# Batch 0's attention ahead of the first x @ w_in, in whole head pairs, with later loads for the rest

## The chip, the cores and the metric

The kernel runs on one core of a Trainium2 chip. The metric is the time of one execution on the device, in microseconds (us). A core has five instruction streams that matter here: PE (TensorE, matmuls and transposes), ACT (ScalarE, exp, tanh and copies), DVE (VectorE, elementwise work), POOL (GpSimd, casts), and SP, which here only issues transfers (DMAs). Each stream runs its instructions strictly in the order in which they were written down; streams wait for one another through semaphores.

## The reference

Attention with a sliding window of 128 and four sink keys, over 4 batches x 8 heads x 768 positions x 64 dims, and then a gated two-layer projection of its output:

```python
scores = scale * np.matmul(q, k.transpose(0, 1, 3, 2))
is_sink = pos[None, :] < 4
in_window = (rel >= 0) & (rel < 128)          # rel = query position - key position
scores = np.where(is_sink | in_window, scores, -1e9)
a = softmax(scores)
x = np.matmul(a, v)                            # then heads side by side: 3072 tokens x 512
h = x @ w_in                                   # 512 x 2048
g = h * (1.0 / (1.0 + np.exp(-beta * h)))
out = g @ w_out                                # 2048 x 512, float32
```

Inputs and output are float32; the kernel computes the matmuls in bfloat16. The gate is computed as h * (1 + tanh(beta * h / 2)), with the factor 0.5 applied to the output.

## The kernel before, in words

**Units and superblocks.** The 3072 tokens are cut into eight superblocks T of 384 (TT), half a batch each. A *unit* n (0 to 31) is the attention of one pair of heads (hp = n % 4) in one half batch; superblock T consists of the units 4T to 4T+3. Even superblocks hold half 0 of a batch, odd ones half 1. A half-1 unit also needs keys of half 0 and the sink keys.

**A unit's chain.** `load` (L392) issues the DMAs of q, k and v into staging tiles. `cast` (L438) makes bfloat16 copies on POOL. For units below XBAR = 12, `transpose_in` (L460) transposes q and k on PE, and DVE copies them out of PSUM into qkT (L475); from unit 12 on, SP issues a transposing DMA instead (L453). `sink_keys` (L478) copies the four sink keys of each head into a block-diagonal tile k_sink, two ACT copies, and `scores_sink` (L488) makes their scores and exps for half-1 units. `scores` (L500) makes the windowed scores in two chunks, each with one exp on ACT (L524). For n below ADDED = 4, large negative tiles (far_a, far_b) are added by a matmul with the identity (L509) in place of the mask; above it, `mask` (L528) multiplies the exps by 0 or 1 on DVE. From unit 12 on, `scores_at_once` (L540) and `mask_at_once` (L567) do both chunks in one. `attend` (L575) multiplies by v, and a column of ones beside v gives the row sums; `normalise` (L609) is a reciprocal and a multiplication on DVE. `transpose_out` (L619) brings the result into xT, below unit 12 through PE and a copy, from 12 on by a transposing DMA on SP (L623).

**Projection.** A *hidden step* i (L663) is four matmuls of 384 columns (L651), for one of the 16 blocks of 128 hidden features of a superblock, then tanh on ACT (L659) and the gate on DVE (L672), which writes g[T % 2]. `project` (L678) is g @ w_out: 16 matmuls of 512 columns for each of a superblock's three row blocks (48 in all, L679), a copy (L687 or L691) and the output DMA (L694). The weights come in 16 pieces of 512 KB, eight of w_in and then eight of w_out, through eight staging tiles (`load_w`, L428), and are cast on POOL (`cast_w`, L433).

**PSUM.** There are eight banks: acc0, acc1, h_ps (two), s_ps (four, of which the third is used for transposes, `tr`, and the fourth for attention outputs, `av`). `hidden_bank` (L640) gives the bank of a hidden step: acc0 and acc1 in turn for superblock 0, all of acc0, acc1 and h_ps for superblock 1, the two of h_ps from superblock 2 on.

**The order of the work.** The program is first written as a list of operations: units 0 to 3, then a loop over steps s from -6. Steps 0 to 31 are the hidden steps of superblocks 0 and 1; steps 32 to 47 (S_P0 to S_PIPE) project superblock 0; from 48 on every step has one hidden step of superblock T + 1 and three project matmuls of T. `FIRST[n]` says at which step unit n enters, and STEPS at how many steps behind that its parts stand (sink 1, scores 2 and 3, attend 5, out 7). Casts and loads of later units hang on the same steps. Then `Prog.order` (L153) goes through the list with an estimated duration for each operation and puts it on its engine at the earliest time its estimate allows, looking at most 160 operations ahead (40 for SP); equal times go by the order of the list. Operations marked `line` (the early loads) keep their order among themselves. The model of transfers adds one duration after another at given rates (`transfer`, L342), and an issue on SP always takes 500 ns in it. What it gives is the fixed order of each engine's instructions.

At the start PE runs 21 matmuls on a tile of ones (`keep_busy`, L718), 14 before the first transposes and 7 behind the cast of unit 0's k.

Of the kernel before, what the change touches and what calls it, by code (L numbers as in the profile page):

```python
# [15 lines left out]
D1 = D + 1  # L16
# [54 lines left out]
class Prog:  # L71
# [13 lines left out]
    FIRST_DMA = 2000.0  # L85
# [67 lines left out]
    def order(self):  # L153
# [10 lines left out]
        dma_free = self.FIRST_DMA  # L164

        def best(e):
# [10 lines left out]
            return max(n.ready, free[e]), n  # L177

        while len(placed) < len(self.nodes):
# [3 lines left out]
            if n.dma is None:  # L183
                n.done = start + n.busy + n.lag
            else:

                dma_free = max(dma_free, start + n.busy) + n.lag
                n.done = dma_free + 2000.0
            n.place = start
# [73 lines left out]
def bass_streamingllm_window__then__act_swish_beta_kernel(  # L263
# [42 lines left out]
    mask_b = sb("mask_b", (128, 512), BF16)  # L306
    far_a = sb("far_a", (128, TT), BF16)
# [13 lines left out]
    g = [sb(f"g{z}", (128, NM, TT), BF16) for z in range(2)]  # L321
    out_sb = [sb(f"out_sb{z}", (128, NOUT), F32) for z in range(4)]
# [19 lines left out]
    def transfer(size, rate):  # L342
        return {"busy": 500.0, "lag": size / rate}
# [9 lines left out]
    def constants():  # L353
# [14 lines left out]

        two = mask_b[:, :].rearrange("p (r x) -> p r x", r=2)
# [21 lines left out]

    def load(n, v_queue="sp"):  # L392
        b, hp, half, pb = place(n)
        t0 = half * TT
        if n < XBAR:
            for name, src in (("q", q), ("k", k)):
# [4 lines left out]
                   dma=f"{name}{pb}_{half}", line=n < WHOLE, **transfer(2 * TT * D * 4, 329))  # L401
        halves = (0, 1) if n >= WHOLE else (half,)
        first, size = (0, 6) if n >= WHOLE else (3 * half, 3)
        for name, src in (("q", q), ("k", k), ("v", v)):
            if name != "v" and n < XBAR:
                continue
            for hh in range(2):
# [6 lines left out]
                   **transfer(size * 128 * D * 4, 220))  # L414
# [13 lines left out]
    def load_w(i):  # L428
        view, src, _ = w_piece(i)
        op("sp", lambda e: e.dma_start(view, src), w=[("wst", i % NW)], dma=f"w{i % NW}",  # L430
           line=True, **transfer(1 << 19, 389))
# [6 lines left out]
    def cast(n):  # L438
        _, _, half, pb = place(n)
        z = n % NQK  # L440
# [4 lines left out]
        for x, name in enumerate("qk"):  # L445
            op("gp", lambda e, x=x, name=name: e.tensor_copy(qk16[z][:, x, :, :, :], view(name)),  # L446
# [5 lines left out]
        if n >= XBAR:  # L452
# [3 lines left out]
               r=[("q16", z), ("k16", z)], w=[("qkT", pb, half)], dma=f"t{pb}{half}",  # L456
               **transfer(2 * TT * 256, 150))


    def transpose_in(n, bank=tr_ps, name_of="tr", eng="dve"):  # L460
        _, _, half, pb = place(n)
        bank16 = bank[:, :].bitcast(BF16)
        z = n % NQK
        for which, name in enumerate("qk"):
# [11 lines left out]
           x=[name_of], w=[("qkT", pb, half)], **(act(768) if eng == "act" else dve(865.0)))  # L476

    def sink_keys(n, eng="act"):  # L478
        pb = place(n)[3]
        for hh in range(2):  # L480
            op(eng, lambda e, hh=hh: (e.copy if eng == "act" else e.tensor_copy)(  # L481
                k_sink[pb][64 * hh:64 * hh + 64, HEAD1 * hh:HEAD1 * hh + NSINK],
                qkT[pb][64 * hh:64 * hh + 64, 0, 1, 0:NSINK]),
               r=[("qkT", pb, 0), ("k_sink", pb), ("k_sink2", pb)],
               w=[("k_sink", pb) if hh == 0 else ("k_sink2", pb)],
               **(act(128) if eng == "act" else dve(180.0)))

    def scores_sink(n, bank, name):  # L488
        pb = place(n)[3]
        op("pe", lambda e: e.matmul(bank[:, 0, 0:TT], k_sink[pb][:, :], qkT[pb][:, 1, 0, :],  # L490
                                    start=True, stop=True),
           r=[("k_sink", pb), ("k_sink2", pb), ("qkT", pb, 1)], w=[f"{name}0"], **pe(TT))
        op("act", lambda e: e.activation(E_sink[n % 2][:, :], bank[:, 0, 0:TT], AF.Exp, bias=0.0,
                                         scale=SCALE),
           x=[f"{name}0"], w=[("E_sink", n % 2)], **act(TT))
# [4 lines left out]
    def scores(n, c, bank, name):  # L500
# [11 lines left out]
        with P.together("pe"):  # L512
            for kb, qb, nq in CHUNKS[half][c]:
                w = 128 * nq
                for hh in range(2):
# [5 lines left out]
                       r=[("qkT", pb, half), ("qkT", pb, kb // 3)], w=[f"{name}{hh}"],  # L521
                       busy=50.0 + w / 4.8, lag=260.0)
                at += w
        op("act", lambda e: e.activation(E[n % 2][:, c, :, 0:at], bank[:, 0:2, 0:at], AF.Exp,  # L524
                                         bias=0.0, scale=SCALE),
           x=[f"{name}0", f"{name}1"], w=[("E", n % 2, c)], **act(768))

    def mask(n, c):  # L528
        if n < ADDED:
# [6 lines left out]
            E[n % 2][:, c, :, 0:w], E[n % 2][:, c, :, 0:w],  # L536
            m[:, first:first + w].unsqueeze(1).to_broadcast([128, 2, w]), ALU.mult),
           r=[("E", n % 2, c), *names], w=[("E", n % 2, c)], **dve(466.0))
# [356 lines left out]
```

## Time and profile before

| | us |
|---|---|
| median of 3 runs | 234.16 |
| lowest, highest | 233.91, 235.1 |
| span of the profiled execution | 234.5 |

The profiled execution gives no time of its own beside its span. The span runs from the first to the last instruction of the profile; it lies 0.3 us above the median of the timed runs and inside their spread.

| engine | busy us | share of the span |
|---|---|---|
| PE | 219.4 | 94% |
| ACT | 144.3 | 62% |
| DVE | 135.2 | 58% |
| POOL | 74.3 | 32% |

DMAs moved 39.76 MB, 170 GB/s over the span. The span in 40 slices of 5.86 us, with the busy share of TensorE and of the DMA engines in tenths (9 is 90% or more), the granted clock in tenths, and what was moved in GB/s:

```profile
PE   4996989999969999999999999999999999999994
PEclk9999999999997999999999999999999999999999
DMA  6999999999699999998999886842220112111012
GB/s 158 269 373 264 318 328 227 321 388 197 147 212 226 177 218 255 203 231 201 215 232 214 182 169 164 160 84 64 62 64 17 45 20 62 45 48 45 19 71 89
```

A line of the timeline has the start, the duration, the engine, the line of the kernel, the operation, output<-input, and how many were merged; in brackets stands how long the engine had been idle and what released it. SPq is SP issuing a transfer.

### The profile page before, as it was taken

The page shows a single profiled execution, that of the slowest core. Times are in us where ns is not written, and L with a number is a line of the kernel's source. Part 1 is how long each engine was busy: PE and PEld are TensorE (multiplying, and loading weights), DVE is VectorE, ACT ScalarE, POOL GpSimd, SP SyncE. Part 2 cuts the span into 40 slices and gives each one's busy share as a digit, 9 for nine tenths or more (in the row PEclk, how much of TensorE's full clock was granted, in tenths as well). Part 3 has the DMA queues.
Part 4 walks back from the last instruction along what each step waited for, and adds up shares of the span by engine and source line. Part 5 has one row for each costly group of instructions (what it writes and reads, how often), then busy time and mean ns, then how long its engine had stood idle before and what let it go on. Part 6 is the DMA issues. An engine that isn't in the chain of part 4 may idle for free.

```text
span 234.5 us, 4406 instructions
## 1 busy us (share of the span) xinstructions
PE 219.4 (94%) x1690; PEld 119.7 (51%) x1714; DVE 135.2 (58%) x261; ACT 144.3 (62%) x249; POOL 74.3 (32%) x134
## 2 busy tenths in 40 slices
PE   4996989999969999999999999999999999999994
PEld 2653545555434555544555555555555555555541
DVE  5374999699632645632667547766656665343300
ACT  2385887697506674755875669767775874555421
POOL 7677777598313223214115343410000000000000
PEclk9999999999997999999999999999999999999999
DMA  6999999999699999998999886842220112111012
GB/s 158 269 373 264 318 328 227 321 388 197 147 212 226 177 218 255 203 231 201 215 232 214 182 169 164 160 84 64 62 64 17 45 20 62 45 48 45 19 71 89
DMA packets 96084, 39.76 MB, mean 170 GB/s; under 512 B 82736, under 2 KB 88896, under 8 KB 96064
## 3 DMA queue, kind: packets, MB, share of 16 engines
q1 hardware_dynamic: 93888, 39.07, 71.0%
q10 hardware_dynamic: 1632, 0.40, 0.8%
q8 instruction: 13, 0.21, 0.4%
q0 software_dynamic: 544, 0.02, 0.2%
q14 instruction: 7, 0.06, 0.1%
HBM read 27.30 MB, written 6.29 MB: 143 GB/s over the span
## 4 chain that ended last, share of the span: by engine, by line
PE 68%; SPq 20%; DMA 8%; issue 2%; POOL 1%; ACT 0%; POOLq 0%; ACTq 0%
PE acc L679 32%; PE h_ps L651 27%; SPq L410 13%; DMA v_stage<-in_v_dram 6%; SPq L399 4%; PE s_ps L554 4%; PE s_ps L604 3%; SPq L430 3%; DMA qkT<-qk 1%; PE s_ps L490 1%; PE s_ps L593 1%; PE h_ps L679 1%; POOL v_aug L449 0%; ACT out_sb L687 0%; POOL qk L446 0%
## 5 line engine op out<-in xcount | busy, mean ns | idle before, releaser
L679 PE MATMUL acc<-w_out,g 128*128 128x512 bf16 x345 | 94.0, 382 | 1.3 <-issue 0.5
L659 ACT ACTIVATE th<-h_ps,beta_half 128x384 f32<-128x384 f32 x104 | 58.9, 581 | 37.7 <-PE h_ps L651 35.8
L651 PE MATMUL h_ps<-xT,w_in 128*128 128x384 bf16 x416 | 79.4, 326 | 0.3 <-issue 0.2
L672 DVE SCALAR_TENSOR_TENSOR g<-th,h_ps 128x384 bf16<-128x384 f32 x104 | 56.0, 552 | 33.6 <-ACT th L659 32.0
L651 PEld LDWEIGHTS h_ps<-xT,w_in 128*128 128x128 bf16 x416 | 39.5, 98 | 30.3 <-DVE g L672 1.5
L679 PEld LDWEIGHTS acc<-w_out,g 128*128 128x128 bf16 x368 | 34.7, 98 | 34.0 <-issue 3.8
L570 DVE TENSOR_TENSOR E<-E,mask_all 128x1536 bf16<-128x1536 bf16 x20 | 19.4, 972 | 29.0 <-ACT E L561 29.0
L561 ACT ACTIVATE E<-s_ps 128x1536 bf16<-128x1536 f32 x20 | 28.9, 1447 | 5.9 <-PE s_ps L554 5.7
L446 POOL CAST qk<-q_stage 128x384 bf16<-128x384 f32 x32 | 18.3, 571 | 33.9 <-DMA qkT<-qk 33.3
L449 POOL CAST v_aug<-v_stage 128x384 bf16<-128x384 f32 x32 | 16.6, 529 | 35.0 <-PE s_ps L604 24.7
L687 ACT ACTIVATE out_sb<-acc 128x512 f32<-128x512 f32 x23 | 13.6, 597 | 14.6 <-PE acc L679 14.2
L651 PE MATMUL acc<-xT,w_in 128*128 128x384 bf16 x96 | 19.1, 327 | 2.6 <-DVE g L672 2.0
L604 PEld LDWEIGHTS s_ps<-v_aug,E 128*128 128x128 bf16 x384 | 17.1, 97 | 5.3 <-ACT E L524 0.7
L604 PE MATMUL s_ps<-v_aug,E 128*128 128x65 bf16 x384 | 19.4, 193 | 0.5 <-ACT E L524 0.4
L614 DVE TENSOR_TENSOR o_norm<-s_ps,rden 128x384 bf16<-128x384 f32 x32 | 17.8, 558 | 2.2 <-DVE rden L612 0.5
L446 POOL CAST qk<-k_stage 128x384 bf16<-128x384 f32 x32 | 18.3, 572 | 2.4 <-DMA k_stage<-in_k_dram 1.7
L659 ACT ACTIVATE th<-acc,beta_half 128x384 f32<-128x384 f32 x24 | 13.7, 580 | 5.9 <-PE acc L651 5.3
L672 DVE SCALAR_TENSOR_TENSOR g<-th,acc 128x384 bf16<-128x384 f32 x24 | 12.9, 547 | 3.8 <-ACT th L659 3.7
L524 ACT ACTIVATE E<-s_ps 128x768 bf16<-128x768 f32 x16 | 12.9, 809 | 2.2 <-PE s_ps L517 2.1
L475 DVE COPY qkT<-s_ps 128x768 bf16<-128x768 bf16 x10 | 9.5, 954 | 5.7 <-PE s_ps L468 5.7
L651 PEld LDWEIGHTS acc<-xT,w_in 128*128 128x128 bf16 x96 | 8.1, 98 | 8.5 <-DVE g L672 3.4
L481 ACT COPY k_sink<-qkT 64x4 bf16<-64x4 bf16 x32 | 6.1, 190 | 10.0 <-DVE qkT L475 9.0
(64 smaller groups left out, 155.0 us busy)
## 6 DMA issues: line engine op xcount, KB each, us to landing
out_dram<-out_sb SPq DMA_DIRECT2D x24, 256.0 KB, 2.3
q_stage<-in_q_dram SPq DMA_DIRECT2D x28, 192.0 KB, 4.2
k_stage<-in_k_dram SPq DMA_DIRECT2D x28, 192.0 KB, 4.2
wst<-in_moe_w_in_dram SPq DMA_DIRECT2D x8, 512.0 KB, 6.3
wst<-in_moe_w_out_dram SPq DMA_DIRECT2D x8, 512.0 KB, 9.1
v_stage<-in_v_dram SPq DMA_DIRECT2D x16, 192.0 KB, 4.2
v_stage<-in_v_dram SPq DMA_DIRECT2D x28, 96.0 KB, 5.3
q_stage<-in_q_dram SPq DMA_DIRECT2D x8, 96.0 KB, 3.3
```

The costliest lines, as they stand in the source:

```text
L410: op(v_queue, lambda e, hh=hh, s=s, name=name: e.dma_start(stage[name][pb][:, hh, first:first + size, :], s), w=[(name + "_stage", pb, x, ...
L446: op("gp", lambda e, x=x, name=name: e.tensor_copy(qk16[z][:, x, :, :, :], view(name)), r=[(name + "_stage", pb, half, hh) for hh in range ...
L449: op("gp", lambda e: e.tensor_copy(v_aug[pb][:, 3 * half:3 * half + 3, :, 0:D], view("v")), r=[("v_stage", pb, half, hh) for hh in range(2 ...
L561: op("act", lambda e: e.activation(E[z][:, :, :, :].rearrange("p c h x -> p c (h x)"), s_ps[:, :, :].rearrange("p (h b) x -> p h (b x)", h ...
L570: op("dve", lambda e: e.tensor_tensor(both, both, mask_all[:, half, :].unsqueeze(1).to_broadcast([128, 2, 768]), ALU.mult), r=[("E", z, 0) ...
L604: last=(x == len(kbs) - 1): e.matmul(av_ps[:, at + hh * D1:at + hh * D1 + D1], E[z][:, c, h2, col:col + 128], v_aug[pb][:, kb, hh, :], sta ...
L614: op("dve", lambda e: e.tensor_tensor(o_norm[o][:, :, :, :].rearrange("p m h d -> p (m h) d"), src[:, :, 0:D], rden[z][:, :].unsqueeze(2). ...
L651: op("pe", lambda e: e.matmul(bank, w_in16[:, c, m * 128:(m + 1) * 128], xT[:, c, T * TT:(T + 1) * TT], start=(c == 0), stop=(c == 3)), r= ...
L659: op("act", lambda e: e.activation(th[i % 3][:, :], bank, AF.Tanh, bias=0.0, scale=beta_half[:, m:m + 1]), x=[name], r=["beta"], w=[("th", ...
L672: op("dve", lambda e: e.scalar_tensor_tensor(g[T % 2][:, m, :], th[i % 3][:, :], 1.0, bank, ALU.add, ALU.mult), r=[("th", i % 3)], x=[name ...
L679: op("pe", lambda e: e.matmul(bank, g[T % 2][:, m, t * 128:(t + 1) * 128], w_out16[:, m, :], start=(m == 0), stop=(m == NM - 1)), r=[("g", ...
L687: op("act", lambda e: e.activation(out_sb[z][:, :], bank, AF.Copy, bias=0.0, scale=0.5), x=[name], w=[("out_sb", z)], **act(NOUT))
```

## The change

It regroups the first part of the program and makes everything behind it later by steps.

- **Order of units.** Units 0, 4, 1, 5, 2, 6, 3, 7 (the two halves of each head pair) all run before the first full hidden step. `turn(n)` gives their place, by which E, rden and o_norm are chosen. The loop over steps begins at 0.
- **Whole pairs.** Pair 0 is still loaded and cast by units (0 and 4). Pairs 1 to 3 are loaded whole (`load_pair`: one DMA for q, one for k, two for v), cast whole (`cast_pair`, into the still unused g[1]) and transposed whole (`turn_pair`: all of k in bank tr, all of q in acc0, one DVE copy each).
- **Sink keys.** One POOL multiplication of the four keys by a 0/1 tile `own_head`, in place of two ACT copies, for every pair. Two more selects at the start fill own_head.
- **Hidden steps** of superblocks 0 and 1 go round all four banks. One hidden step is begun before the last part of xT is there, in place of two.
- **Slots.** Units 8 to 11 enter at steps 31, 34, 37 and 40 (before 22, 26, 30, 34), units 12 on two steps later than before. Units 4 to 7 have no slots any more. The last chunk of scores of units 4 to 7 is in h_ps, as for 0 to 3, and their sink scores are in acc1.
- **Loads.** All loads of the first units go through SP (before, the v of units 0 and 1 went through ACT's queue). The order on SP is batch 0, w_in, w_out, units 8 to 13; 14 and 15 hang on the casts of 12 and 13, and whole pairs of batches 2 and 3 are asked for when the unit two before them is cast (before, four before them).
- **Casts.** The eight casts of w_in stand behind the casts of batch 0, those of w_out at step 0, ahead of the casts of units 8 and 9. The two DMAs of the sinks' v stand behind the casts of pair 0's units.
- **The ordering model.** At most seven transfers under way (DEPTH): an eighth issue waits for the landing of the one seven before it. Rates and issue times of transfers are changed, a transposing DMA's issue takes 1250 or 1400 ns in the model, and FIRST_DMA is 1300.
- **keep_busy**: 10 matmuls in place of 21.

The core of the diff:

```diff
-FIRST = {4: -6, 5: -4, 6: -2, 7: 1, 8: 22, 9: 26, 10: 30, 11: 34}
-FIRST.update({n: 42 + 4 * (n - 12) for n in range(12, NU)})
+FIRST = {8: 31, 9: 34, 10: 37, 11: 40}
+FIRST.update({n: 44 + 4 * (n - 12) for n in range(12, NU)})
...
-    FIRST_DMA = 2000.0
+    FIRST_DMA = 1300.0
+    DEPTH = 7
...
+            start = max(n.ready, free[e])
+            if n.dma is not None and len(landing) >= self.DEPTH:
+                start = max(start, landing[-self.DEPTH])
+            return start, n
...
+    def load_pair(hp):
+
+        for name, src in (("q", q), ("k", k)):
+            s = src[0, 2 * hp:2 * hp + 2, :, :].rearrange("h (p c) d -> p h (c d)", c=6)
...
+        for hh in range(2):
+            s = v[0, 2 * hp + hh, :, :].rearrange("(c p) d -> p c d", p=128)
...
+    def cast_pair(hp):
+        z = hp % 2
+        for x, name in enumerate("qk"):
+            op("gp", lambda e, x=x, name=name: e.tensor_copy(
+                pair16[z][x][:, :, :, :], stage[name][hp][:, :, :, :].rearrange("p h c d -> p c h d")),
...
+    def turn_pair(hp):
+        z = hp % 2
+        for x, (bank, name) in ((1, (tr_ps, "tr")), (0, (acc[0], "acc0"))):
+            bank16 = bank[:, :].bitcast(BF16)
+            with P.together("pe"):
+                for c in range(6):
+                    op("pe", lambda e, c=c, x=x, bank16=bank16: nc.tensor.transpose(
...
+            op("dve", lambda e, dst=dst, src=src: e.tensor_copy(dst, src), x=[name],
+               w=[("qkT", hp, half) if x else ("qT", hp, half) for half in range(2)], **dve(865.0))
...
-    def sink_keys(n, eng="act"):
+    def sink_keys(n):
         pb = place(n)[3]
-        for hh in range(2):
...
+        op("gp", lambda e: e.tensor_tensor(
+            k_sink[pb][:, 0:2 * HEAD1].rearrange("p (h x) -> p h x", h=2)[:, :, 0:NSINK],
+            qkT[pb][:, 0, 1, 0:NSINK].unsqueeze(1).to_broadcast([128, 2, NSINK]), own_head[:, :, :],
+            ALU.mult), r=[("qkT", pb, 0), "own_head"], w=[("k_sink", pb)], busy=120.0, lag=100.0)
...
-        k = i % 2 if i < NM else i % 4 if i < S_P0 else 3 - i % 2
+        k = i % 4 if i < S_P0 else 3 - i % 2
...
-    for n in range(4):
-        load(n, "act" if n < 2 else "sp")
+    load(0)
...
     load(4)
...
+    for hp in range(1, 4):
+        load_pair(hp)
+    for x in range(8):
+        load_w(x)
     cast(0)
-    cast(1)
+    cast(4)
...
-    keep_busy(14, 215.0)
...
+    keep_busy(10, 215.0)
+    transpose_in(0)
+    cast_pair(1)
+    transpose_in(4, acc[0], "acc0")
+    for n in (0, 4, 1, 5, 2, 6, 3, 7):
+        hp, half = n % 4, n // 4
+        if half == 0:
+            if 0 < hp < 3:
+                cast_pair(hp + 1)
+            if hp:
+                turn_pair(hp)
+            sink_keys(n)
         scores(n, 0, s_ps, "s")
+        if half == 0 and hp:
+            scores_sink(n + 4, acc[1], "acc1")
...
+        if n == 6:
+            for i in range(8):
+                cast_w(i)
+        if n == 3:
+            for i in range(8, 16):
+                load_w(i)
+            for n_ in range(8, 14):
+                load(n_)
+            with P.together("pe"):
+                for c in range(3):
+                    hidden_matmul(0, c)
...
-    casts = {FIRST[n - 2] + 1: n for n in range(6, NU) if n not in (8, 9)}
-    for s in range(-6, S_END + NM):
+    casts = {FIRST[n - 2] + 1: n for n in range(10, NU)}
+    for s in range(S_END + NM):
...
-            if n >= XBAR and n % 8 >= 4 and n + 4 < NU:
-                load(n + 4)
...
+            if n in (12, 13):
+                load(n + 2)
+            if n >= XBAR + 2 and n % 8 in (6, 7, 0, 1) and n + 2 < NU:
+                load(n + 2)
...
-        if s == FIRST[7] + 1:
+        if s == 0:
 
-            for x in (8, 9, 10, 11):
+            for x in range(8, 16):
                 cast_w(x)
             cast(8)
...
             cast(9)
```

More of the change, by code (lines that the diff above doesn't have):

```diff
@@ L340, in dve, with transfer @@
         return {"busy": t, "lag": 140.0}
-    def transfer(size, rate):
-        return {"busy": 500.0, "lag": size / rate}
+    def transfer(size, rate, issue=525.0):
+        return {"busy": issue, "lag": size / rate}
     def select(out_ap, in_ap, patt, cmp, fill, base, cm, r, w):
@@ L783, in bass_streamingllm_window__then__act_swish_beta_kernel @@
             if step in ("a", "b") and n < XBAR:
-                scores(n, "ab".index(step), *((h_ps, "h") if n < 8 and step == "b" else (s_ps, "s")))
+                scores(n, "ab".index(step), s_ps, "s")
                 later.append(lambda n=n, step=step: mask(n, "ab".index(step)))
```

175 lines of the change are left out of this document (76 added, 99 removed).

## The prediction

> **What bounds the kernel now.** I read the chain that ended last first, as shares and then in order of time; then busy time and clock by stage; then single engines inside the stages.
>
> ```profile
> PE 68%; SPq 20%; DMA 8%; issue 2%; POOL 1%; ACT 0%; POOLq 0%; ACTq 0%
> ```
>
> The chain in order of time:
>
> ```profile
> 45.02 1.21 SPq L410
> 46.27 1.73 SPq L410
> ...
> 58.38 1.48 SPq L410
> 66.60 3.48 DMA qkT<-qk
> 71.21 0.85 PE acc L679 x2
> ```
>
> Up to 70 us the end hangs on SP's queue and the transfers (the 28%); from 71 us on it hangs on TensorE alone. Columns of the next view: stretch in us, its length, then busy us (instructions) of PE, PEld, DVE, ACT, POOL, then granted clock, DMA share, GB/s.
>
> ```profile
> 8.70:19.00 10.30, 9.48 (x120) 5.78 (x119) 6.19 (x11) 8.69 (x19) 6.56 (x10) 1.00 1.13 324
> 19.00:42.00 23.00, 19.73 (x202) 11.26 (x199) 20.05 (x40) 16.02 (x29) 16.77 (x26) 1.00 1.03 283
> 42.00:56.00 14.00, 13.60 (x107) 7.91 (x105) 12.18 (x25) 12.34 (x25) 12.16 (x17) 1.00 1.01 325
> 56.00:67.86 11.86, 11.70 (x104) 5.95 (x105) 8.34 (x17) 4.80 (x10) 5.46 (x11) 1.00 0.77 172
> 67.86:70.12 2.26, 0.00 (x1) 0.00 (x0) 0.36 (x1) 0.00 (x0) 0.11 (x1) 1.00 1.23 228
> 70.12:74.80 4.68, 4.67 (x20) 1.72 (x21) 0.46 (x1) 2.17 (x3) 1.03 (x3) 0.64 1.30 229
> 74.80:234.50 159.70, 154.88 (x1123) 83.66 (x1142) 84.56 (x157) 98.81 (x165) 25.86 (x48) 1.00 0.60 125
> ```
>
> The last row is the pipelined part: 97% PE, full clock. It starts when the projection of superblock 0 is done, at 74.80. So the change is worth what it moves that boundary, plus what it breaks behind it. Ahead of the boundary time is lost in three places: 19 to 42 us (superblock 0's hidden steps, among attention, round two banks), the PE gap of 2.26 us, and the half clock behind the gap (mean 0.64 over 4.68 us). The gap on PE:
>
> ```profile
> 67.53 0.33 PE L631 MATMUL s_ps<-ident,o_norm 128*128 128x128 bf16 x3
> 70.13 0.34 PE L490 MATMUL s_ps<-qkT,k_sink 128*128 128x384 bf16 x1 [2.27 <-DMA qkT<-qk]
> ```
>
> PE waits for unit 12's transposing DMA, which SP issued only at 66.60, behind a row of loads. SP puts later output transposes off too:
>
> ```profile
> 66.60 1.32 SPq L453 DMA_TRANSPOSE qkT<-qk  x1
> ...
> 93.89 1.26 SPq L623 DMA_TRANSPOSE xT<-o_norm  x1
> ```
>
> Unit 12's o_norm was written at 77.06 to 77.62, so its transpose stood 16 us in SP's queue. Unit 19's was ready at 120.4 and issued at 132.28; superblock 4's hidden matmuls begin at 137.77, and 96.7 us follow from there.
>
> ACT in a unit of the first stage:
>
> ```profile
> 14.33 0.42 ACT L481 COPY k_sink<-qkT 64x4 bf16<-64x4 bf16 x2
> 14.75 0.81 ACT L524 ACTIVATE E<-s_ps 128x768 bf16<-128x768 f32 x1
> 15.46 0.81 ACT L524 ACTIVATE E<-h_ps 128x768 bf16<-128x768 f32 x1
> 16.15 0.49 ACT L635 COPY xT<-acc 128x384 bf16<-128x384 bf16 x1
> 16.69 0.42 ACT L481 COPY k_sink<-qkT 64x4 bf16<-64x4 bf16 x2
> ```
>
> There is no gap: 2.36 us a unit, and ACT sets it.
>
> **The change, part by part.** Durations are distances between starts where instructions follow closely.
>
> *All attention of batch 0 first (stage A).* Four pairs, each a half-0 and a half-1 unit. Per pair: ACT four exps at 0.70, one sink exp 0.37, two copies at 0.5: 4.2. The two key copies (0.42) go; with them it would be 4.6. DVE: two copies into qkT at 0.87, two reciprocals and normalisations at 0.70, two masks at 0.47 (31.31, POOL idle beside it) to 0.92 (26.68, beside a POOL cast): 4.1 to 5.0. PE: half 0 0.34 in, 0.66 far tiles, 0.54 scores, 0.57 attend, 0.17 out; half 1 0.34, 0.16 sink, 0.54, 0.62, 0.17: 4.1. POOL: two casts of 384 columns lie 0.45 apart, so 0.9 for a 768-column one, three of them, and the key multiplication: 2.9. Three engines stand at 4.1 to 5.0, so I take 4.75, nearer DVE's upper end, since POOL casts through all of the stage. From the first qkT copy (8.62, left there) four pairs end at 27.6. The last unit's transposes and ACT copy add 1.2 (20.02 to 20.87 is 0.85, and a wait): 28.8. Superblock 0 needs only the seventh unit, 2.4 earlier, while PE still owes 1.8 to the eighth: PE is free for hidden steps from about 28.3.
>
> *Loads of the stage.* Batch 0 is 4.72 MB; the trace moved 4.69 MB by 17.6 us (158, 269, 373 GB/s), so pair 3 lands near 17.7, about 5 us before its turn. w_in, 4.19 MB at the next slices' 264 to 328, is in by 31.5; its last quarter is needed twelve steps (7.8) after 28.3, which leaves 3.6 for the cast of 1.04. The v loads of units 0 and 1 move from ACT's queue to SP's, four issues of 0.5, but whole pairs need 20 loads where there were 32: SP is 8 issues (4 us or more) better off. The pieces of q and k double in length; no gain is counted for that.
>
> *Start.* Two more selects on POOL, 0.3 to 0.45 each, lie ahead of its 0.84 us wait for the v_sink fill: 0. The v_sink DMAs (1.36 us of POOL) may now follow the casts: 0 to 1.4 earlier or later for the first cast; 0. Eleven of 21 filler matmuls go. Those of 256 columns came 0.213 us apart between 5.61 and 7.74 (0.83 ns a column, later matmuls 0.42), so the array was at half speed until about 8.4. With less filler this may last. Nothing lost if not; if through all of pair 0, 4.1 of PE becomes 8.2 against 4.75: 3.4. I take 1.0, as the recorded half-clock stretch at 70 us (3.4 us long, so 1.7 lost) is nearest, and part of it lies beside waits for loads.
>
> *Key multiplication on POOL.* Not in the trace: between 0.10 (memset of 1 column) and 0.35 (128 columns); 0.25. One a pair, POOL at 2.9 of 4.75 covers it. It waits for a DVE copy with the next pair's casts behind it; these have about 1.8 us a pair to spare. Uncovered it is 4 x 0.25 = 1 us.
>
> *x @ w_in round four banks.* 32 steps of four matmuls, 0.65 a step in the dense rows (46.49 to 49.09 is four steps in 2.60): 20.8. ACT (0.48) and DVE (0.47) stay under it. Before, superblock 0's sixteen steps, with four units, took 19 to 42 us. I add 0.5 at the start, where banks are still shared with the last unit.
>
> *Projection of superblock 0, now with units 8 to 11 whole.* 48 x 0.216 = 10.4; units at 0.34 + 0.54 + 0.45 + 0.17 = 1.5, four: 6.0; unit 12's sink and scores 0.9: 17.3. Such a mix ran with 0.16 us free in 11.86 (56.00 row); I add 0.5. What would be late next are the loads: w_out, 4.19 MB behind w_in at 321 to 388, is in near 44; units 8 to 12, 2.95 MB at 230 to 260, near 56. Unit 8 enters near 49, its load in by 46.5 and cast by 48.5, behind w_out's casts on POOL; unit 12's transpose can go at 58, its scores come near 66. The gap and its half clock have 8 us of cover.
>
> *Loads and slots later.* Units 12 on start two steps later in a program that stands earlier: a whole pair is asked for eight steps before its cast (16 before), about 13 us at 1.65 a step. Landing took 4 to 9 us in this trace, so 0; without the cover, see the second rival. SP's transposes no longer stand behind the loads of units 24 to 27. PE work behind the boundary is the same: 159.7.
>
> Sum: 28.3 + 1.0 + 20.8 + 0.5 + 17.3 + 0.5 + 159.7 = 228.1 of span against 234.5. The median (234.16) lies 0.3 under this span, so about **228.0**. With ends: stage A at 4.1 or 5.7 a pair, start 0 to 3.4: 224.2 to 234.0 (225.2 with the 1.0 kept).
>
> A rule of the Trainium skill about the gap: TensorE: Matmul & The Clock Gate, "What's actually happening", gives an idle window of about 3.4 us ahead of half rate. Here 2.27 us were enough, and the row decides. By the page only the gap itself would be saved, an estimated 1.7 us less.
>
> **The rivals.**
> 1. Stage A is slower: the pair's chain runs through four engines, and a pair at 5.7 with 2 us of half speed gives 28.3 + 3.8 + 2.0 + 198.8 - 0.3 = 232.6. For it: masks at 0.92 beside POOL. Against: units followed at 2.36 with ACT full.
> 2. The other side: late loads move the wait to superblock 4. It cannot start before unit 19's output is transposed, and 96.7 us follow. Units 12 to 19 need 6.6 us each; unit 12 is done near 69.5, unit 19 near 116. A whole pair is 1.18 MB per four steps; the slice at 59 to 64 us moved 147 GB/s, 8.0 us a pair. At 8.5 a unit the last ends near 137.5, superblock 4 starts near 142, and the end is at 238.4. It decides from about 7.8 a unit. For it: DMA share over 1 from 70 to 100 us. Against: units came every 6.1 us there, with loads for units 24 to 27 between them.
> 3. No gain: DMA keeps its pace, units 12 to 19 end when they did, and PE's lead is spent waiting: 233 to 235.
> 4. The clock falls through the hidden steps. Rotating through banks leaves small pauses on PE; if half of the 20.8 us ran at half clock, +10: 238. Against: 42 to 56 us, already round four banks, held 1.00. The page named above states this in "A second HAM failure mode: psum-queue depth-cycling"; the trace does not bear it out.
>
> **How the numbers follow.** Forecast 0.52 (225.5 to 231.5); better, pairs at 4.2 and no half clock, 0.10 (223 to 225.5); rival 1 0.15; rival 3 0.07; rival 2 0.12; rival 4 0.04. Under 233.0 is faster by 0.5%, about what a measurement can tell: faster 0.77, same 0.07, slower 0.16. The range 223.5 to 235.0 leaves out the slower ones and a little of the better case.
>
> **What would show it.** Right: projection of superblock 0 ends near 68 to 69, the 32 hidden steps take about 21 us from 28 to 29, no PE gap over 1 us before 70 us, and 159 to 160 us follow. Wrong: PE waiting for xT at superblock 3 or 4, half clock in the first 30 us, pairs over 5.5 us.

## The result, and the profile after

| | before | after |
|---|---|---|
| median (lowest to highest), us | 234.03 (233.84 to 235.1) | 242.35 (239.43 to 243.29) |
| span of the profiled execution, us | 234.5 | 241.4 |
| superblock 0's hidden steps begin in full, us | 19.0 | 33.2 |
| projection of superblock 0 ends, us | 74.8 | 74.0 |
| from there to the end, us | 159.7 | 167.4 |

The change made the kernel slower: ratio 1.027 [1.021, 1.034], against a forecast of 228.0 and a range of 223.5 to 235.0. The ratio goes by the two faster of the four runs (239.43 and 241.58); the profiled execution is one of the other two (243.12). All profiled executions from here on have a time of their own, 1.7 to 2.0 us above their span.

So both halves of the forecast failed: the boundary came 0.8 us earlier, not 6.4, and what follows became 7.7 us longer. First the windows of after, cut at its own stages (columns as before: stretch, length, busy us and instructions of PE, PEld, DVE, ACT, POOL, then clock, DMA share, GB/s):

```profile
8.70:33.20 24.50, 20.28 (x247) 13.10 (x246) 18.08 (x30) 16.59 (x27) 19.44 (x29) 1.00 1.09 366
33.20:55.36 22.16, 22.16 (x133) 13.05 (x131) 17.13 (x32) 18.02 (x32) 13.77 (x19) 0.92 0.94 278
55.36:74.00 18.64, 18.55 (x171) 9.12 (x168) 13.82 (x28) 8.83 (x13) 8.52 (x19) 1.00 0.65 126
74.00:101.40 27.40, 27.40 (x226) 15.09 (x225) 16.07 (x29) 18.23 (x27) 9.81 (x20) 1.00 1.16 238
101.40:137.00 35.60, 30.32 (x215) 15.23 (x214) 17.16 (x32) 19.21 (x28) 8.39 (x18) 0.93 0.84 196
```

The rows are batch 0's attention, the 32 hidden steps of superblocks 0 and 1, the projection of superblock 0 with units 8 to 11, and then the pipeline. The last row is where the pipeline loses: PE is idle for 5.28 of 35.60 us, and the clock is 0.93. Before, no stretch behind the boundary looked like this. The timeline of PE in after names the two waits:

```profile
103.58 0.99 PE L709 MATMUL h_ps<-xT,w_in 128*128 128x384 bf16 x5 [1.48 <-DMA xT<-o_norm]
133.16 1.78 PE L709 MATMUL h_ps<-xT,w_in 128*128 128x384 bf16 x5 [3.80 <-DMA xT<-o_norm]
```

At superblock 3 and again at superblock 4, the first hidden step has its first three matmuls done and stands before the fourth, whose part of xT has not landed. Behind the second wait five matmuls take 1.78 us instead of 0.99: half clock, granted for 6.8 us from 132.3 on. Lost are 1.48 + 3.80 in waits and, of the 6.8, what lies behind the wait at half speed, (6.8 - 0.86) / 2 = 3.0: 8.3 together, where the pipeline grew by 7.7. (It is no full balance: behind the boundary PE was idle for 4.8 us before and for 8.5 after.)

Why the part of xT was late is in SP's queue, of after:

```profile
119.27 1.22 SPq L681 DMA_TRANSPOSE xT<-o_norm  x1
...
122.22 1.53 SPq L444 DMA_DIRECT2D v_stage<-in_v_dram  x2
123.80 1.86 SPq L444 DMA_DIRECT2D q_stage<-in_q_dram  x2
125.71 1.40 SPq L444 DMA_DIRECT2D k_stage<-in_k_dram  x2
127.15 1.30 SPq L444 DMA_DIRECT2D v_stage<-in_v_dram  x2
128.49 2.61 SPq L681 DMA_TRANSPOSE xT<-o_norm  x1
```

and in DVE's timeline:

```profile
122.19 0.56 DVE L672 TENSOR_TENSOR o_norm<-s_ps,rden 128x384 bf16<-128x384 f32 x1
```

This is unit 19's o_norm. It was ready at 122.75, but its transpose stood 5.7 us behind issues of loads for batch 3, went out at 128.49 and landed 4.6 us later. (The chain of waits links this transpose to an o_norm that starts at 128.34. That is unit 20's, and it ends at 128.90, after the issue at 128.49: a releaser that ends later than what it is said to release is a wrong guess, and the queue's own view tells the truth.)

The transpose was late only for this order of PE. In before it went out 3.8 us later than here, at 132.28, after 11.9 us in the queue; but PE came to superblock 4 only at 137.6, with more project matmuls ahead of it, and didn't wait. In after PE stood there from 129.4 on.

### The profile page after: what moved, and what is told of

The parts are those of the page before. It is cut to its first block, busy times and chain, and to the rows that moved or that the text cites. A ratio compares the mean times of both kernels' runs of the same rounds, so it can differ in the third digit from the quotient of the medians.

```text
span 241.4 us, 4374 instructions
## 1 busy us (share of the span) xinstructions
PE 224.4 (93%) x1703; PEld 121.8 (50%) x1703; DVE 137.4 (57%) x257; ACT 141.6 (59%) x221; POOL 74.2 (31%) x143
## 4 chain that ended last, share of the span: by engine, by line
PE 86%; DVE 6%; DMA 3%; ACT 3%; issue 1%; DVEq 0%; ACTq 0%
PE acc L737 34%; PE h_ps L709 31%; PE s_ps L662 5%; PE acc L709 4%; PE s_ps L612 4%; DMA xT<-o_norm 3%; ACT E L582 2%; DVE E L593 2%; PE s_ps L575 1%; PE h_ps L737 1%; PE s_ps L651 1%; DVE o_norm L672 1%; PE s_ps L529 1%; PE s_ps L548 1%; DVE v_sink L360 1%; PE s_ps L567 1%
## 5 line engine op out<-in xcount | busy, mean ns | idle before, releaser
L717 ACT ACTIVATE th<-h_ps,beta_half 128x384 f32<-128x384 f32 x112 | 64.6, 581 | 59.6 <-PE h_ps L709 57.4
L737 PE MATMUL acc<-w_out,g 128*128 128x512 bf16 x368 | 99.0, 381 | 0.1
L709 PE MATMUL h_ps<-xT,w_in 128*128 128x384 bf16 x448 | 90.1, 334 | 5.3 <-DMA xT<-o_norm 5.3
L730 DVE SCALAR_TENSOR_TENSOR g<-th,h_ps 128x384 bf16<-128x384 f32 x112 | 61.4, 552 | 51.1 <-ACT th L717 48.8
L709 PEld LDWEIGHTS h_ps<-xT,w_in 128*128 128x128 bf16 x448 | 44.1, 100 | 42.7 <-DMA xT<-o_norm 6.1
L737 PEld LDWEIGHTS acc<-w_out,g 128*128 128x128 bf16 x368 | 33.4, 98 | 31.2 <-issue 3.7
L507 POOL CAST qk<-q_stage 128x384 bf16<-128x384 f32 x26 | 13.7, 528 | 44.8 <-DMA q_stage<-in_q_dram 26.4
L582 ACT ACTIVATE E<-s_ps 128x768 bf16<-128x768 f32 x16 | 13.1, 818 | 18.0 <-PE s_ps L575 17.3
L662 PEld LDWEIGHTS s_ps<-v_aug,E 128*128 128x128 bf16 x384 | 17.6, 99 | 6.6 <-DVE E L593 1.7
L672 DVE TENSOR_TENSOR o_norm<-s_ps,rden 128x384 bf16<-128x384 f32 x32 | 17.8, 557 | 1.1
L507 POOL CAST qk<-k_stage 128x384 bf16<-128x384 f32 x26 | 14.4, 553 | 12.4 <-DMA k_stage<-in_k_dram 12.3
L709 PE MATMUL acc<-xT,w_in 128*128 128x384 bf16 x64 | 12.6, 339 | 0.0
L670 DVE RECIPROCAL rden<-s_ps 128x6 f32<-128x6 f32 x32 | 6.1, 191 | 8.8 <-PE s_ps L662 8.6
L612 PE MATMUL s_ps<-qkT 64*128 64x256 bf16 (+2 forms) x144 | 10.4, 261 | 0.0
L651 PE MATMUL s_ps<-v_sink,E_sink 128*128 128x130 bf16 x48 | 9.7, 226 | 0.5 <-ACT E_sink L551 0.5
```

Of the source, the lines that this page charges most:

```text
L507: op(eng, lambda e, x=x, name=name: e.tensor_copy(qk16[z][:, x, :, :, :], view(name)), r=[(name + "_stage", pb, half, hh) for hh in range( ...
L582: op("act", lambda e: e.activation(E[turn(n) % 2][:, c, :, 0:at], bank[:, 0:2, 0:at], AF.Exp, bias=0.0, scale=SCALE), x=[f"{name}0", f"{na ...
L612: op("pe", lambda e, kb=kb, bank=bank, qb=qb, at=at, nq=nq, rows=rows: e.matmul(s_ps[:, bank, 128 * at:128 * (at + nq)], qkT[pb][rows, kb ...
L662: last=(x == len(kbs) - 1): e.matmul(av_ps[:, at + hh * D1:at + hh * D1 + D1], E[z][:, c, h2, col:col + 128], v_aug[pb][:, kb, hh, :], sta ...
L672: op("dve", lambda e: e.tensor_tensor(o_norm[o][:, :, :, :].rearrange("p m h d -> p (m h) d"), src[:, :, 0:D], rden[z][:, :].unsqueeze(2). ...
L709: op("pe", lambda e: e.matmul(bank, w_in16[:, c, m * 128:(m + 1) * 128], xT[:, c, T * TT:(T + 1) * TT], start=(c == 0), stop=(c == 3)), r= ...
```

## The experiments

Each is compared with runs of the kernel before on the same chip. Times in us; the ratio is to before, with a 95% interval.

**1. The old numbers of the ordering model in the changed kernel (e1_transfer_model_before).** Kernel: the changed one, all else kept.

```diff
-    FIRST_DMA = 1300.0
-    DEPTH = 7
+    FIRST_DMA = 2000.0
+    DEPTH = 9999
...
-    def transfer(size, rate, issue=525.0):
+    def transfer(size, rate, issue=500.0):
+        issue, rate = 500.0, {240: 150, 280: 150, 250: 220, 300: 329, 330: 329, 380: 389, 350: 389}[rate]
```

> The changed kernel with the ordering model's transfer numbers of the kernel before (no DEPTH, 150 GB/s for transposing DMAs, 500 ns an issue); program list unchanged. Order theory (the fixed PE order puts the first hidden steps of superblocks 3 and 4 just where the model lets xT land, and the real landing is 10 to 14 us behind the model, so PE waits 1.5 and 3.8 us and then runs 6.8 us at half clock): with these numbers the projection of superblock 3 comes ahead of superblock 4's hidden steps, the two waits go, the part from superblock 2's first hidden step to the end falls from 167.3 to 159 to 161 us, total near 234 to 236. Transfer theory (loads of batches 2 and 3 take the time they take, whatever the order): the waits only move, total 239 to 244.

Measured: 234.6, ratio 1.0016 [0.9975, 1.0056], span 232.8. No wait for xT, no half clock; boundary 72.3, then 160.5. The whole slowdown goes with these numbers, though they execute nothing: they only decide where instructions stand. Counted in the traces, 192 project matmuls stand ahead of superblock 4's first hidden step in e1 and 158 in after. The 34 that moved behind it are 34 x 0.216 = 7.3 us of work that could have run while PE waited there for 3.8 us; that the count decides is argued here, and experiment 7 speaks against it. SP's queue alone doesn't decide either. In e1:

```profile
116.48 0.56 DVE L673 TENSOR_TENSOR o_norm<-s_ps,rden 128x384 bf16<-128x384 f32 x1
...
125.70 3.56 SPq L682 DMA_TRANSPOSE xT<-o_norm  x2
...
135.65 1.47 PE L710 MATMUL h_ps<-xT,w_in 128*128 128x384 bf16 x8
```

Unit 19's o_norm was done at 117.04 and its transpose, the first of the two, went out at 125.70. It stood 8.7 us in the queue, longer than the 5.7 of after, and PE didn't wait, since it came to superblock 4 only at 135.65.

**2. No loads of batch 3 (e2_no_batch3_loads).** The changed kernel:

```diff
-            if n >= XBAR + 2 and n % 8 in (6, 7, 0, 1) and n + 2 < NU:
+            if n >= XBAR + 2 and n % 8 in (6, 7, 0, 1) and n + 2 < 24:
```

> The changed kernel without the loads of batch 3 (units 24 to 31 compute on batch 2's q, k and v again; this leaves out 4.7 MB of transfers). Both the order theory and the transfer theory expect unit 19's output transpose to be issued 4 to 6 us sooner (no loads ahead of it in SP's queue) and the wait at superblock 4 to shrink from 3.8 us to under 1, with its half clock: total 234 to 237. The slot theory (units stand two steps too late, loads have no part) expects the wait to stay at 3 us or more and the total within 2 us of 241.

Measured: 236.34, ratio 1.0034 [0.9996, 1.0073]. Unit 19's transpose went out at 122.42, right behind its o_norm, and the wait at superblock 4 is gone. The one at superblock 3 stayed (1.99 us at 101.73, then half clock):

```profile
122.42 1.19 SPq L681 DMA_TRANSPOSE xT<-o_norm  x1
...
101.73 1.07 PE L709 MATMUL h_ps<-xT,w_in 128*128 128x384 bf16 x5 [1.99 <-DMA xT<-o_norm]
```

So it is those loads that unit 19's transpose stands behind. Their transfers are gone as well as their issues, so this run doesn't say which of the two held it up.

**3. The filler matmuls back (e3_filler_back).** The changed kernel:

```diff
-    keep_busy(10, 215.0)
+    keep_busy(14, 215.0)
     transpose_in(0)
+    keep_busy(7, 200.0, [("k16", 0)])
```

> The changed kernel with the 21 filler matmuls of the kernel before (14, and 7 behind the cast of unit 0's k). Order and transfer theories: half speed ends near 9 us in place of 16.3, the attention of batch 0 ends 1 to 3 us sooner (superblock 0's hidden steps begin near 31 in place of 33.2), but unit 19's output lands only 0 to 1.5 us sooner, so the wait at superblock 4 grows and the total falls by less than 1.5. Start theory (the slow start is what costs): total falls by 3 us or more.

Measured: 240.08, ratio 1.0187 [1.0103, 1.0271]; full clock from 7.3 us (16.3 in after), yet the full hidden steps start at 32.9 (33.2 in after), not near 31, and those of superblock 1 at 42.9; in e2, at full clock only from 13.7, they start at 42.6. Half speed in the first pairs costs next to nothing. The wait at superblock 4 didn't grow, as expected, but shrank to 2.55 us, with 3.4 us of half clock behind it, and the median fell by 2.3: both misses. What e3 saves against after ahead of the boundary (superblock 1's steps start at 45.0 there) is another stretch: in after, half clock is granted for 3.4 us from 33.4, 1.7 us lost just as the dense matmuls begin; e3 and e2 don't have it.

**4. Loads of whole pairs four units ahead again (e4_early_pair_loads).** The changed kernel:

```diff
-            if n >= XBAR + 2 and n % 8 in (6, 7, 0, 1) and n + 2 < NU:
-                load(n + 2)
+            if n >= XBAR and n % 8 >= 4 and n + 4 < NU:
+                load(n + 4)
```

> The changed kernel with the rule of before for whole-pair loads (asked for when the unit four before them is cast, in place of two). If it is the lateness of these loads that makes units 12 to 19 late: unit 19's output transposed 3 us sooner or more, total 236 to 238. If the loads stand in SP's queue ahead of the output transposes either way (order and transfer theories): unit 12's and 13's outputs are transposed later than now (83.2 and 90.5), unit 19's about where it is (within 2 us of 128.5), total 240 to 244.

Measured: 241.71, ratio 1.0255 [1.016, 1.0349], with waits for xT of 1.23 and 3.67 us; unit 12's transpose went out at 92.4, unit 19's at 129.9. The change of when loads are asked for isn't the cause.

**5. The kernel before with only the new numbers (e5_before_with_new_model).**

```diff
-    FIRST_DMA = 2000.0
+    FIRST_DMA = 1300.0
+    DEPTH = 7
...
+            if n.dma is not None and len(landing) >= self.DEPTH:
+                start = max(start, landing[-self.DEPTH])
...
-               **transfer(2 * TT * 256, 150))
+               **transfer(2 * TT * 256, 240, 1400.0))
...
-               r=[("o_norm", z)], w=[("xT", T, hp)], dma=f"x{z}", **transfer(TT * 256, 150))
+               r=[("o_norm", z)], w=[("xT", T, hp)], dma=f"x{z}", **transfer(TT * 256, 280, 1250.0))
```

and the rates of loads, weights and output as in the change.

> The kernel before with only the changed kernel's transfer numbers in its ordering model (DEPTH 7, the new rates and issue times, FIRST_DMA 1300); units, loads, slots and banks as before. In the order that comes out, 109 and 151 project matmuls stand ahead of the first hidden steps of superblocks 3 and 4 on PE (138 and 188 in the kernel before, 107 and 158 in the changed one). Order theory: PE then waits for xT at superblock 3 or 4 for 2 us or more, as in the changed kernel, and the kernel is slower than before by 2 to 8 us: 236 to 242. Rival (the changed program needs its own order, the numbers themselves are harmless or better): 232 to 235, no wait over 1 us.

Measured: 243.77, ratio 1.0424 [1.0332, 1.0515]. This is above the expected 236 to 242: the attention order of before, and the same loss. PE in e5:

```profile
126.76 0.65 PE L657 MATMUL h_ps<-xT,w_in 128*128 128x384 bf16 x3
131.95 1.78 PE L657 MATMUL h_ps<-xT,w_in 128*128 128x384 bf16 x5 [4.54 <-DMA xT<-o_norm]
```

PE also waits 1.56 us for a qkT transpose at 96.21. The boundary is at 71.3, the rest takes 169.9; 151 project matmuls stand ahead of superblock 4. With e1 this is the pair that settles where the loss comes from.

**6. Slack for the landing of xT (e6_slack_for_xt).** The changed kernel, with the model told that the transposes of units 12 to 19 land 6 us later:

```diff
+                if n.dma[0][0] == "x" and n.dma[1] <= 32:
+                    n.done += 6000.0
```

> The changed kernel with all its transfer numbers, and 6 us added in the ordering model to the landing of the output transposes of units 12 to 19 alone: 144 and 174 project matmuls stand ahead of superblocks 3 and 4 in place of 107 and 158, nothing else is meant to change. Order theory: no wait over 1 us at superblock 3, under 1.5 us at superblock 4, 4 to 7 us less than the changed kernel: 234.5 to 237.5. Rival (DEPTH and the rates do harm through the order of SP's queue, not through PE's): waits stay, 240 to 243.

Measured: 239.79, ratio 1.0221 [1.0139, 1.0302]. A miss. Both waits for xT are gone, but the order that came out has another at 113.36, where PE waits 2.22 us for DVE's mask, with half clock behind it, and the stretch at 33 us is there too; 164.8 follow the boundary. Mending one due time doesn't give the old order back.

**7. Which of the numbers (e9_depth_off_alone, e10_old_rates_alone).** Both are the changed kernel. e9 takes the limit of seven transfers away and keeps the new rates; e10 keeps the limit and takes the old rates, issue times and FIRST_DMA.

```diff
# e9
-    DEPTH = 7
+    DEPTH = 9999
# e10
-    FIRST_DMA = 1300.0
+    FIRST_DMA = 2000.0
...
+        issue, rate = 500.0, {240: 150, 280: 150, 250: 220, 300: 329, 330: 329, 380: 389, 350: 389}[rate]
```

> The changed kernel without DEPTH, its new rates kept. 121 and 152 project matmuls stand ahead of superblocks 3 and 4 on PE (107 and 158 in the changed kernel, 140 and 192 in the first experiment). Order theory, by these counts: superblock 3 gains 14 matmuls, 3.0 us, so its wait goes, superblock 4 does not, so PE still waits 2 us or more there and runs at half clock behind it: 238 to 242. If DEPTH alone does the harm: 234 to 236, as in the first experiment.

> The changed kernel with the rates and issue times of before, and DEPTH 7 kept. The counts are the same 121 and 152. Order theory: as the run without DEPTH, a wait of 2 us or more at superblock 4, 238 to 242. If the rates (280 GB/s for output transposes in place of 150) alone do the harm: 234 to 236.

Measured: e9 241.63, ratio 1.0319 [1.0262, 1.0376], waits for xT of 5.12 us at superblock 3 and 1.01 at superblock 4. e10 235.41, ratio 1.0037 [0.9998, 1.0076]. So it is the new rates, issue times and FIRST_DMA, which e10 takes back together; the limit of seven is not needed for the loss. I had gone by the count of project matmuls, and there both are misses. e9 has 121 ahead of superblock 3, 14 more than after, and waits there for 5.12 us instead of 1.48. e10 is the other: 152 ahead of superblock 4, as few as in e9, and no wait for xT in its trace. What differs is SP's queue, here of e10:

```profile
116.03 1.21 SPq L682 DMA_TRANSPOSE xT<-o_norm  x1
117.29 1.17 SPq L445 DMA_DIRECT2D q_stage<-in_q_dram  x2
118.50 1.13 SPq L445 DMA_DIRECT2D k_stage<-in_k_dram  x2
119.68 1.22 SPq L682 DMA_TRANSPOSE xT<-o_norm  x1
```

Two entries of loads stand between the transposes of units 18 and 19, not the row of after, and they issue at 0.6 us each; unit 19's o_norm was done at 116.37, 6.4 us sooner than in after, its transpose went out 3.3 us later, and superblock 4 began at 123.3. That trace is the fastest execution of e10 (232.79); the others have granted clocks of 0.978 to 0.993 against its 1.000, so most of them lose the clock somewhere that no trace of mine shows.

**8. No masks in batch 0's attention (e7_model_and_added8).** e1 with far tiles instead of masks for units 4 to 7 too:

```diff
-    ADDED, FAR = 4,
+    ADDED, FAR = 8,
```

> The first experiment's kernel (transfer numbers of before) with ADDED = 8, so that units 4 to 7 also get their mask as a matmul with the identity on PE and DVE has no mask to multiply while batch 0's attention runs. If the masks beside POOL's casts (two of them took 2.25 and 2.10 us in the changed kernel, 0.94 elsewhere) made that stage long: the last o_norm comes 1.5 to 3 us sooner (34.2 now) and the total 1 to 3 us lower, 232 to 233.5. If the chain of the last units through PE, ACT and DVE did, whatever the masks cost: under 1 us sooner, 234 to 235.

Measured: 232.65, ratio 0.9932 [0.9895, 0.9969]: faster than before. The last o_norm of batch 0 is done at 31.8 (34.2 in e1), the boundary at 70.1 (72.3), and 160.5 follow, all at full clock.

**9. The key multiplication alone (e8_before_pool_sink_keys).** The kernel before, with own_head and the multiplication on POOL in place of the two ACT copies:

```diff
-        for hh in range(2):
...
+        op("gp", lambda e: e.tensor_tensor(
+            k_sink[pb][:, 0:2 * HEAD1].rearrange("p (h x) -> p h x", h=2)[:, :, 0:NSINK],
...
```

> The kernel before with only the sink keys changed: one POOL multiplication in place of two ACT copies. ACT sets the pace of units 0 to 3 at 2.36 us with these copies in it: without them 1.9 to 2.2 us a unit, the fourth unit's o_norm 0.5 to 1.4 us sooner (19.96 now). Beyond 20 us SP's queue and the transfers decide, so the total stays within 1 us of before: 233 to 235.

Measured: 233.16, ratio 0.9949 [0.9922, 0.9976]. Units 0 to 3 end at 13.0, 15.3, 17.7 and 20.0 us, where they ended in before (12.9, 15.2, 17.6, 20.0): the expected gain in pace is a miss, and ACT, though it showed no gap, didn't set it. In the traces the difference lies at 70 us: unit 12's transpose goes out at 65.1 instead of 66.6, and PE doesn't stop. What lowered the median stays open, since by its clock the profiled execution of before is not a typical one (see the last step below).

**10. The same without the reorganisation, and with the filler (e11_before_sink_added8, e12_added8_filler).** e11 is e8 with ADDED = 8. e12 is e7 with the filler of e3.

```diff
# e11, on e8, and e12, on e7
-    ADDED, FAR = 4,
+    ADDED, FAR = 8,
# e12
-    keep_busy(10, 215.0)
+    keep_busy(14, 215.0)
     transpose_in(0)
+    keep_busy(7, 200.0, [("k16", 0)])
```

> The kernel before with the sink keys on POOL and ADDED = 8, both parts of the best kernel so far but with the old order of units, loads and slots. If batch 0's attention ahead of the hidden steps is worth something by itself, this is slower than the last run of this call by 0.5 to 1.5 us: 232.5 to 234. If only the sink keys and the masks were: equal to it within 0.4 us, 231.5 to 233.

> The best kernel so far (the changed one with the old transfer numbers and ADDED = 8) with the 21 filler matmuls of before. Half speed ends near 7 to 9 us in place of 12.4. From the run with the filler alone (attention of batch 0 shorter by 0 to 0.5 us): 231.5 to 232.7, equal to the run without filler within 0.5 us. If the early half speed costs what the prediction gave it, 1.0 us less: near 231.5.

Measured: e11 233.61, ratio 0.997 [0.9935, 1.0004]; e12 232.32, ratio 0.9926 [0.9897, 0.9955], the lowest median of the study, below both before and after (e7 is not told apart from it). Full clock from 7.6 us on bought 0.3 against e7 at the boundary (69.8 against 70.1). Between e11 and e12 the medians are 1.3 us apart on one chip, and twelve runs each hardly overlap (232.37 to 234.8, 231.83 to 232.65): about that much is what the rest of the change is worth together (the order of units, whole pairs, loads, slots and banks), with the old numbers behind it. No run takes these apart.

## Why the prediction was wrong, step by step

**"PE work behind the boundary is the same: 159.7."** This failed by 7.7, and it is what turned the sign. The part on loads and slots says that SP's transposes no longer stand behind the loads of units 24 to 27; I costed the moved loads and didn't cost the new numbers of the ordering model at all. They decide the place of every transpose, load, hidden step and project matmul behind 70 us. e1 and e5 show that they carry the loss in either kernel (1.0016 without them in the changed one, 1.0424 with them in the old one), e9 and e10 that the rates, issue times and FIRST_DMA do, without the limit of seven. The first transposes did come earlier, unit 12's at 83.2 instead of 93.9; unit 19's stood behind loads all the same.

**The second rival** named the right place, superblock 4, and the wrong mechanism. It priced units that need more than 7.8 us each for want of load bandwidth, 238.4. (From unit 12 to unit 19 are seven units, not eight: 69.5 + 7 x 8.5 = 129.0, and its own terms then end at 229.9.) Units 12 to 19 ended at 78.5 to 122.7, 6.3 us each, so loads kept up; what was late was one transpose in SP's queue, with nothing on PE placed to fill the wait. Which part the place of the loads on SP has and which the place of hidden steps on PE stays open: e2 and e10 speak for the queue, e6 took the waits away through the model's landing time and still lost elsewhere. The queue alone it is not: unit 19's transpose stood 8.7 us in e1, 11.9 in before and 14.1 in e7, and PE waited for none of them. As far as these runs show, what the new numbers lost is the fit of the two orders, SP's and PE's.

**The third rival** had a part of it. Units 12 to 19 ended no sooner than in before (77.6 to 120.4 there), and PE's lead at superblock 4 (128.7 against 137.6) went into waiting. But it had a wait use up the gain, not a loss with half clock behind the wait.

**Stage A, 28.3 and 1.0 for the start.** Full hidden steps began at 33.2. The o_norms of the second halves of pairs 0 to 3 were done at 17.4, 24.1, 28.3 and 34.2. Two things:

- From 8.62 pair 0 took 8.7 us, not 4.75, since I took four pairs at their pace and forgot the first pair's latency: its two units run one after the other through casts, transposes, copy, scores, exp and attend, with little but pair 1's transposes and far tiles to fill the engines. (Its first qkT copy started at 7.57, so by the prediction's own mark it took 9.8.) By the rows, the key multiplication adds to it; no run takes this apart. I gave it 1.8 us a pair to spare; in pair 0 there was none. POOL in after:

```profile
8.62 0.20 POOL L541 TENSOR_TENSOR k_sink<-qkT,own_head 128x8 bf16<-128x8 bf16 x1 [1.49 <-DVE qkT L536]
8.77 0.49 POOL L507 CAST qk<-q_stage 128x384 bf16<-128x384 f32 x1
```

  POOL stood still for 1.49 us with unit 4's casts behind the multiplication. Its own time, 0.20, was priced well (0.25).
- Pairs 1 to 3 took 5.6 us each, at the upper end (5.7) that I kept for rival 1 and not the 4.75 I chose. The masks are the difference. DVE in after:

```profile
20.55 2.25 DVE L593 TENSOR_TENSOR E<-E,mask_b 128x768 bf16<-128x768 bf16 x2
...
24.91 0.55 DVE L593 TENSOR_TENSOR E<-E,mask_b 128x768 bf16<-128x768 bf16 x1
...
30.77 2.10 DVE L593 TENSOR_TENSOR E<-E,mask_b 128x768 bf16<-128x768 bf16 x2
```

  The slow pairs of masks ran beside POOL casts (of w_in, in the last), 1.05 to 1.13 each; the one at 24.91, with hardly any cast beside it, took 0.55. One at 26.07 took 0.64, though a cast of w_in started within it, and that cast took 1.36 instead of 1.03. e7, without masks, needs 4.9 a pair. The Trainium skill says in GPSIMD Engine Reference, "1. Specifications", that GpSimd's SBUF interfaces are shared with VectorE and contended by VectorE instructions with two SBUF inputs, as a mask is; the rows agree, though no run took the casts away. I had both row values (0.47 and 0.92) and weighed them as DVE's busy sum; but a mask stands between exp and attend, in a chain that PE waits for (0.73 us in front of the last attends).

**Start and clock.** Half speed lasted until 16.3 us, nearly through all of pair 0, a case that the prediction priced at 3.4, and cost under 0.5 (e3, e12): PE wasn't what stage A waited for. (The clock column has no entry before 16.3 and shows 1.00; six transposes took 0.85 us at 14.15 and 0.51 at 17.98.) The half clock came where I hadn't looked, at 33.4, on the first dense steps. PE was busy 4.25 of the 6 us before 34, with no wait over 0.73 us. That is not enough to explain it: in the same 6 us PE was busy 4.06 in e1 and e10 and 4.25 in e2 and e3, and none of them lost the clock. It added 1.7 to the 32 hidden steps: 22.2 against 20.8 + 0.5. In e7 and e12 these steps ran without it; e7's first two stages behind batch 0 and its last stretch:

```profile
31.00:51.30 20.30, 20.30 (x128) 12.28 (x129) 17.01 (x32) 17.84 (x32) 14.92 (x20) 1.00 1.03 331
51.30:70.10 18.80, 18.71 (x172) 9.20 (x171) 13.59 (x28) 8.94 (x13) 8.38 (x19) 1.00 0.82 180
133.50:230.60 97.10, 92.91 (x633) 49.38 (x631) 48.91 (x91) 56.90 (x90) 6.90 (x16) 1.00 0.26 67
```

**What held.** The 0.65 a step round four banks (20.3 for what is left of 32 steps from 31.0 on in e7), no lost clock from the rotation itself (rival 4), the loads of batch 0 and the weights in time, no PE gap before 70 us. The projection stage is 0.8 to 1.0 over 17.3 + 0.5. The boundary by my terms was 28.3 + 1.0 + 21.3 + 17.8 = 68.4; measured 33.2 + 22.2 + 18.6 = 74.0. All three signs of being wrong that the prediction names came: PE waiting for xT, half clock in the first 30 us, and pairs over 5.5 us.

**"The median lies 0.3 under this span."** This step was wrong too. All later profiled executions have times 1.7 to 2.0 above their spans; by that, the profiled execution of before took 236.2 or more and was 2 us slower than the median. Its granted clock is 0.992, from the half clock behind the gap at 70 us. Of 67 later executions of before, 16 show a clock of 0.993 or less (median 237.2) and the other 51 one of 0.998 to 1.000 (median 234.4). About 2 of the 6.4 us that I took off were by this estimate losses that the median doesn't contain; a span of 228.1 would have been a time of about 229.8. With the old numbers back, e1's 234.6 against 228.0 is then accounted for: 3.9 at the boundary (72.3 against 68.4), 0.8 behind it and 2.0 between span and time.

## What to carry to other kernels

Where a kernel's instruction order is planned from estimates, a change of the estimates is a change of the program, and it has to be costed like one: look at which transfer each engine will stand before, and what work is left to fill that wait. Price a stage that is new at the front as the latency of its first item plus the pace of the rest, and an elementwise operation by the slower of its rows when casts run beside it all through the stage. Before taking a gap in one trace as gain, find out whether the median execution has it: compare the profiled execution's time, and its clock, with the timed runs.

## What the hardware showed that was not expected

- The clock fell after less idling than I had thought needed: 3.4 us of half clock behind e2's wait of 1.99 us, 6.8 behind 3.80 us in after, and 3.4 at the end of a stage whose last waits of PE were 0.73 us and less. Waits of 1.48 us (after, superblock 3) and 1.33 us (e3) had none behind them, and neither had the same stage in e1, e2, e3 and e10, with last waits of 0.74 to 0.93 us. The Trainium skill, in TensorE: Matmul & The Clock Gate, "What's actually happening", tells of an idle window of about 3.4 us that is free-running; the lengths of 3.4 and 6.8 us agree with windows of that size, the 1.99 us of idling ahead does not agree with a whole idle window.
- With the changed order, the first full clock came at 7.3 and 7.6 us with 21 filler matmuls (e3, e12) and mostly at 12.4 to 16.7 us with 10; in e9 it came at 7.8, and 3.4 us of half clock followed from 11.3 on. It cost under 0.5 us, in a stage that PE didn't limit.
- A transposing DMA of xT held SP for 1.2 to 1.3 us in most rows, and for 2.6 us at 128.49 in after, behind a row of loads. Those at 90.54 and 97.92, also behind rows of loads, took 1.23 and 1.27, so what stretches an issue isn't shown.
